# Moving a table's angles to integers on one engine and its sines ahead of the products, in an FFT filter followed by a feed-forward layer

## The chip, the cores and the metric

The kernel runs on one core of a Trainium2 chip. The metric is the device time of one execution in microseconds (us). "Span" is the time from the first to the last instruction in the profiler's records; the device time is longer than the span, most often by 2.0 or 2.1 us.

## The reference, cut to what matters

```python
def _attn_ref(x, filt_r, filt_i):              # x: 8 x 3008 x 256, filters 1505 x 256
    X = np.fft.rfft(x, axis=1)
    F = (filt_r + 1j * filt_i)[None, :, :]
    return np.fft.irfft(X * F, n=x.shape[1], axis=1).astype(np.float32)

def _moe_ref(x, w_in, w_out, beta):            # 24064 tokens, 256 -> 2048 -> 256
    h = x @ w_in
    g = h * (1.0 / (1.0 + np.exp(-beta * h)))
    return (g @ w_out).astype(np.float32)
```

The kernel does the transforms as matrix products with tables of sines and cosines, in two steps each way. It builds the tables on the chip at its start. `t2`, the second table, is the large one: 24 blocks of 64 columns in five copies (cosine, cosine, sine, sine, minus cosine). The first batch item goes through the whole transform (the "head", 36 us), and then the **main stage** begins: feed-forward matmuls on TensorE with a SiLU on ScalarE for each of 752 steps, into which the transforms of batch items 1 to 7 are woven.

## The kernel before

The angles of half 0 of `t2` are computed on VectorE and those of half 1 on GpSimd, in fp32 turns, and rounded with the usual add-and-subtract of a large constant:

```python
ROUND_C = 1.5 * (2**23)
def angles(h, eng):
    u = setup.tile([P, NH, M], F32, ...); r = setup.tile([P, NH, M], F32, ...)
    eng.tensor_tensor(u[:], ka[...half h, broadcast...], kb[...broadcast...], ALU.add)
    eng.tensor_scalar(r[:], u[:], ROUND_C, ROUND_C, ALU.add, ALU.subtract)
    eng.tensor_tensor(u[:], u[:], r[:], ALU.subtract)

def t2_part(h, part):                       # all on ScalarE, 128x768 or 2 x 128x384
    if part == 0:   nc.scalar.activation(t2[:, ks_, 2, :], u[:], ACT.Sin, scale=TWO_PI)
    elif part == 1: nc.scalar.activation(r[:], u[:], ACT.Abs)
    else:           # two cosines, as sines of r with a bias of half pi
        ...
angles(0, nc.vector)
angles(1, gp)
```

`first1(i, on_act)` multiplies four rows of `x` for one of eight blocks and evacuates two psum tiles into `a_t`, each by ScalarE or VectorE; `warm(n)` is n matmuls on zeros that keep TensorE busy. ScalarE does half 1 of the table only among the products:

```python
for i in range(2):
    first1(i, (True, True))
    warm(2 if i == 0 else 8)
t2_part(0, 0)
first1(2, (False, False)); warm(2)
for part in (1, 2): t2_part(0, part)
first1(3, (False, False)); warm(2)
t2_sin(0, nc.vector); t2_more(0)            # copies and negation on VectorE
first1(4, (False, False)); warm(2)
first1(5, (True, True)); warm(2)
first1(6, (True, True)); warm(1)
first1(7, (False, True))
...                                          # turn_a: transposes of a_t, evacuated
product(0)
TAB = (1, 2, 5, 6, 8, 9)
for i in range(NK // 2 + FLAG):              # NK // 2 = 12 products, 2 multiplies each
    if 0 < i < NK // 2: product(i)           # VectorE: nc.vector.tensor_tensor(..., ALU.mult)
    ...
    if i < 3:  t2_part(1, i)
    if i in TAB: table3(...)                 # a table's transposes, evacuated
    if i == 3:
        t2_more(1)
        for h in range(1, 4): load_wout(h)   # weights of the feed-forward layer
        load_x(1, X_HALVES[2:], xs[1])       # second halves of batch item 1
        ...
    if i >= FLAG: inverse3(i - FLAG)
```

Two places in the main stage turn out to matter. The work woven into it is placed by step number, and the filter loads `uf` are issued on the same queue (SyncE) as the stores of the results, which leave from a pool of three staging buffers:

```python
ostp = pool("ostp", 3)
...
at = place(9, 14, units[J // 4 :], per=9)
place(at + 1, at + 1, [lambda: a2_read(1)] + uf(JG, NK), per=9)   # steps 15 and 16: 8 filter loads
...
if fb == NFB - 1:                                   # a block of 512 rows is done
    for h, a in enumerate(acc):
        if h * per % 2 == 0:
            ost = ostp.tile([P, 2, D], F32, name="ost", tag="ost")
        on_act = h == 0 and i < 6 or last and h % 2 == 0
        evac(ost[...], a[:], on_act)                # ScalarE or VectorE
        eng = nc.scalar if last and h >= 2 else nc.sync
        store(..., ost[...], eng)
```

## Time and profile before

| | before |
|---|---|
| device time, median of 3 | 782.55 us (782.0 to 783.15) |
| span of the profiled execution | 780.9 us |
| busy share: TensorE, ScalarE, VectorE, GpSimd | 99%, 76%, 50%, 19% |
| first multiply of the products starts | 16.27 us |
| last (24th) multiply starts | 32.00 us |
| first SiLU (start of the main stage as ScalarE sees it) | 36.38 us |
| last SiLU starts | 775.68 us |

### The profile page before, as it was taken

The page shows a single profiled execution, that of the slowest core. Times are in us where ns is not written, and L with a number is a line of the kernel's source. Part 1 is how long each engine was busy: PE and PEld are TensorE (multiplying, and loading weights), DVE is VectorE, ACT ScalarE, POOL GpSimd, SP SyncE. Part 2 cuts the span into 40 slices and gives each one's busy share as a digit, 9 for nine tenths or more (in the row PEclk, how much of TensorE's full clock was granted, in tenths as well). Part 3 has the DMA queues.
Part 4 walks back from the last instruction along what each step waited for, and adds up shares of the span by engine and source line. Part 5 has one row for each costly group of instructions (what it writes and reads, how often), then busy time and mean ns, then how long its engine had stood idle before and what let it go on. Part 6 is the DMA issues. An engine that isn't in the chain of part 4 may idle for free.

```text
span 780.9 us, 15549 instructions
## 1 busy us (share of the span) xinstructions
PE 772.5 (99%) x6111; PEld 549.0 (70%) x6111; DVE 392.8 (50%) x644; ACT 594.3 (76%) x922; POOL 145.3 (19%) x144
## 2 busy tenths in 40 slices
PE   9999999999999999999999999999999999999998
PEld 5767667766777667876668766787677776776665
DVE  8847846746446563475635746277452761500101
ACT  6987886886678867787677876778767787677776
POOL 8522501420013100231002310024000330000000
PEclk9999999999999999999999999999999999999999
DMA  9978674517801186022850239412371114100101
GB/s 187 245 188 229 155 211 134 127 68 202 222 28 68 69 209 195 29 81 96 196 167 28 96 114 183 148 56 81 120 206 43 61 68 128 55 29 28 55 28 55
DMA packets 84185, 91.46 MB, mean 117 GB/s; under 512 B 4498, under 2 KB 74276, under 8 KB 83154
## 3 DMA queue, kind: packets, MB, share of 16 engines
q1 hardware_dynamic: 81008, 73.95, 30.9%
q0 software_dynamic: 2816, 16.26, 10.7%
q8 instruction: 48, 0.79, 0.4%
q10 hardware_dynamic: 288, 0.26, 0.1%
q14 instruction: 25, 0.20, 0.1%
HBM read 57.16 MB, written 46.66 MB: 133 GB/s over the span
## 4 chain that ended last, share of the span: by engine, by line
PE 95%; DVE 2%; ACT 1%; issue 1%; DVEq 0%
PE acc L877 42%; PE hps L835 41%; PE ps L626 3%; PE ps L551 3%; PE ps L674 2%; PE ps L648 2%; PE pw L187 1%; DVE qb_t L451 0%; DVE a_t L109 0%; ACT a L107 0%; DVE q_t L660 0%; PE pz L543 0%; DVE q_t L663 0%; DVE p_t L659 0%; ACT z_t L107 0%
## 5 line engine op out<-in xcount | busy, mean ns | idle before, releaser
L844 ACT ACTIVATE gT<-hps,beta_sb 128x512 bf16<-128x512 f32 x752 | 515.4, 687 | 174.0 <-PE hps L835 163.3
L877 PE MATMUL acc<-wout_sb,gT 128*128 128x256 bf16 x3008 | 451.4, 272 | 0.0
L835 PE MATMUL hps<-y,win_sb 128*128 128x512 bf16 (+8 forms) x1730 | 447.8, 351 | 0.3 <-ACT gT L844 0.3
L877 PEld LDWEIGHTS <-gT 128*128 128x128 bf16 x3008 | 285.7, 98 | 128.1 <-ACT gT L844 0.2
L835 PEld LDWEIGHTS <-win_sb 128*128 128x128 bf16 x1730 | 164.9, 98 | 24.7 <-issue 0.6
L664 POOL TENSOR_TENSOR v_t<-p_t,q_t 128x512 bf16<-128x512 f32 x84 | 106.7, 1270 | 387.7 <-DVE q_t L663 377.6
L109 DVE COPY ost<-acc 128x512 f32<-128x512 f32 (+1 forms) x88 | 56.2, 677 | 193.2 <-PE acc L877 188.8
L109 DVE CAST a<-ps 96x512 bf16<-96x512 f32 x96 | 65.9, 687 | 86.3 <-PE ps L626 84.8
L111 DVE TENSOR_SCALAR y<-ps 128x376 bf16<-128x376 f32 (+1 forms) x119 | 63.8, 544 | 61.2 <-PE ps L551 61.2
L659 DVE TENSOR_TENSOR p_t<-ps,frr 128x512 f32<-128x512 f32 x84 | 58.1, 691 | 29.9 <-PE ps L648 28.0
L663 DVE TENSOR_TENSOR q_t<-ps,fri 64x512 f32<-64x512 f32 x84 | 58.3, 694 | 1.2
L660 DVE SCALAR_TENSOR_TENSOR q_t<-ps,fri 64x512 f32<-64x512 f32 x84 | 57.5, 684 | 1.1
L551 PEld LDWEIGHTS <-zz 96*128 96x128 bf16 x512 | 35.3, 97 | 28.9
L107 ACT ACTIVATE z<-ps 128x512 bf16<-128x512 f32 x84 | 49.5, 589 | 0.6 <-PE ps L674 0.6
L626 PE MATMUL ps<-xg,t 94*96 94x512 bf16 x112 | 41.9, 381 | 0.1
L551 PE MATMUL ps<-t,zz 96*128 96x94 bf16 x448 | 36.7, 204 | 0.0
L674 PE MATMUL ps<-v_t,t 128*128 128x256 bf16 x168 | 32.1, 273 | 1.0 <-DVE q_t L663 1.0
L648 PE MATMUL ps<-a,t 128*128 128x256 bf16 x168 | 32.1, 273 | 0.0
L118 POOL DMA_DIRECT2D xg<-in_x_dram x22 | 12.0, 550 | 100.1 <-PE acc L877 96.8
L648 PEld LDWEIGHTS <-t 128*128 128x128 bf16 x168 | 15.8, 98 | 14.4
L626 PEld LDWEIGHTS <-t 94*96 94x96 bf16 x112 | 13.6, 123 | 11.9
L674 PEld LDWEIGHTS <-t 128*128 128x128 bf16 x168 | 16.1, 98 | 7.8 <-DVE q_t L663 1.8
(121 smaller groups left out, 196.8 us busy)
## 6 DMA issues: line engine op xcount, KB each, us to landing
out_dram<-ost SPq DMA_DIRECT2D x80, 256.0 KB
d<-a SPq DMA_DIRECT2D x28, 384.0 KB
a<-d SPq DMA_DIRECT2D x28, 384.0 KB
d<-z SPq DMA_DIRECT2D x28, 384.0 KB
zz<-d SPq DMA_DIRECT2D x28, 384.0 KB
xg<-in_x_dram POOLq DMA_DIRECT2D x6, 1280.0 KB, 10.1
frr<-in_filt_r_dram SPq DMA_DIRECT2D x12, 256.0 KB
out_dram<-ost SPq DMA_DIRECT2D x18, 128.0 KB
```

What stands on the lines that cost most here:

```text
L109: nc.vector.tensor_copy(dst, src)
L111: nc.vector.tensor_scalar_mul(dst, src, scale)
L551: nc.tensor.matmul(ps[:, e, :NP], lhsT=zz[:, jj + e, dc * P : (dc + 1) * P], rhs=tab[:], start=True, stop=True,)
L626: nc.tensor.matmul(ps[:KP], lhsT=t1[:], rhs=s["x"][:, 2 * i : 2 * i + 2, :], start=True, stop=True)
L648: nc.tensor.matmul(ps[:, e, :], lhsT=t2[:, k0 + e, 3:5, :].rearrange("p c k -> p (c k)"), rhs=s["a2"][g][:, kk + e, :], start=True, stop=True,
L659: nc.vector.tensor_tensor(p_t[:], ps[:], frr[:, ks_, :], ALU.mult)
L663: nc.vector.tensor_tensor(q_t[:M], ps[M:P], fri[M:P, ks_, :], ALU.mult)
L664: nc.gpsimd.tensor_tensor(v_t[:], p_t[:], q_t[:], ALU.add)
L674: nc.tensor.matmul(ps[:, e, :], lhsT=t3[:, k0 + e, :], rhs=v_t[:, e, :], start=True, stop=True)
L835: nc.tensor.matmul(hps[:, pos - t0 : pos - t0 + ln], lhsT=win_sb[:, dc, fb * P : (fb + 1) * P], rhs=ys[b][:, dc, n0 : n0 + ln], start=(dc ...
L844: nc.scalar.activation(gT[:, :tn], hps[:, :tn], ACT.Silu, scale=beta_sb[:, fb : fb + 1])
L877: nc.tensor.matmul(acc[tb // per][:, tb % per, :], lhsT=g_[:, tb * P : (tb + 1) * P], rhs=wout_sb[:, f_, :], start=(f_ == 0 and tb % per = ...
```

## The change

The intent: take the angle work off slow GpSimd, make it cheaper on VectorE (the remainder of a turn is one bit operation on integers), and have all sines of the table done before the products, so that ScalarE evacuates for the products undisturbed. GpSimd gets the copies. Cut to its core:

```diff
+TURN = 2**22
...
-    angles(0, nc.vector); angles(1, gp)          # add, round, subtract
+    for h in range(2):
+        u = setup.tile([P, NH, M], I32, name="u", tag=f"u{h}")
+        nc.vector.tensor_tensor(u[:], ka[...], kb[...], ALU.add)
+        nc.vector.tensor_scalar(u[:], u[:], TURN - 1, None, ALU.bitwise_and)
...
-            nc.scalar.activation(t2[:, ks_, 2, :], u[:], ACT.Sin, scale=TWO_PI)
+            nc.scalar.activation(t2[:, ks_, 2, :], u[:], ACT.Sin, scale=TWO_PI / TURN, bias=pi[:])
-            nc.scalar.activation(r[:], u[:], ACT.Abs)
+            nc.scalar.activation(r[:], u[:], ACT.Abs, scale=1.0 / TURN, bias=half[:])
...
+    first1(0, (True, True));   warm(2);  t2_part(0, 0)
+    first1(1, (False, False)); warm(8);  t2_part(0, 1); t2_part(0, 2); t2_copy(0, 3, 2)
+    ...                                            # keep, on GpSimd
+    t2_copy(0, 0, 1)
     first1(2, (False, False)); warm(2)
+    first1(3, (True, True));   warm(2)
+    nc.vector.tensor_scalar_mul(t2[:, :NH, 4, :], t2[:, :NH, 1, :], -1.0)
+    t2_part(1, 0)
+    first1(4, (False, False)); warm(1)
+    t2_part(1, 1)
+    first1(5, (False, True));  warm(1)
+    first1(6, (False, True));  first1(7, (False, True))
...
+    t2_part(1, 2)
+    t2_copy(1, 3, 2); t2_copy(1, 0, 1)             # GpSimd
+    gp.tensor_tensor(t2[:, NH:, 4, :], zeros, t2[:, NH:, 1, :], ALU.subtract)
...
-        if i < 3: t2_part(1, i)
-            table3(1 + n // 2, 2 - 2 * (n % 2), n % 2 == 0 or n == 5)()
+            table3(1 + n // 2, 2 - 2 * (n % 2), n % 2 == 0)()
```

More of the change, by code (lines that the diff above doesn't have):

```diff
@@ L242 @@
     hm = fixed("hm", -0.5 * math.pi)
+    pi = fixed("pi", -math.pi)
+    half = fixed("half", -0.5)
     ms = small("ms")
     nc.vector.tensor_scalar(ms[:], q_p[:], float(J), j_p[:], ALU.mult, ALU.add)
-    nc.vector.tensor_scalar_mul(ms[:], ms[:], 1.0 / S)
+    nc.vector.tensor_scalar_mul(ms[:], ms[:], float(TURN) / S)
     off2 = small("off2")
-    nc.vector.tensor_scalar(off2[:], c_p[:], -0.25, 0.25, ALU.mult, ALU.add)
+    nc.vector.tensor_scalar(off2[:], c_p[:], -0.25 * TURN, 0.75 * TURN, ALU.mult, ALU.add)
     ka = setup.tile([P, NK], F32, name="ka", tag="ka")
@@ L257 @@
     NH = NK // 2
-    us, rs = [], []
-    def angles(h, eng):
-        u = setup.tile([P, NH, M], F32, name="u", tag=f"u{h}")
-        r = setup.tile([P, NH, M], F32, name="r", tag=f"r{h}")
-        eng.tensor_tensor(
+    us = []
+    for h in range(2):
+        u = setup.tile([P, NH, M], I32, name="u", tag=f"u{h}")
+        nc.vector.tensor_tensor(
             u[:],
@@ L268, in angles @@
         )
-        eng.tensor_scalar(r[:], u[:], ROUND_C, ROUND_C, ALU.add, ALU.subtract)
-        eng.tensor_tensor(u[:], u[:], r[:], ALU.subtract)
+        nc.vector.tensor_scalar(u[:], u[:], TURN - 1, None, ALU.bitwise_and)
         us.append(u)
-        rs.append(r)
+    rs = [setup.tile([P, NH, M], F32, name="r", tag=f"r{h}") for h in range(2)]
     def t2_part(h, part):
@@ L277, in t2_part @@
         if part == 0:
-            nc.scalar.activation(t2[:, ks_, 2, :], u[:], ACT.Sin, scale=TWO_PI)
+            nc.scalar.activation(
+                t2[:, ks_, 2, :], u[:], ACT.Sin, scale=TWO_PI / TURN, bias=pi[:]
+            )
         elif part == 1:
-            nc.scalar.activation(r[:], u[:], ACT.Abs)
+            nc.scalar.activation(r[:], u[:], ACT.Abs, scale=1.0 / TURN, bias=half[:])
         else:
@@ L285, in t2_part, with t2_copy @@
                 )
-    def t2_sin(h, eng):
+    def t2_copy(h, dst, src):
         ks_ = slice(h * NH, (h + 1) * NH)
-        eng.tensor_copy(t2[:, ks_, 3, :], t2[:, ks_, 2, :])
-    def t2_more(h):
-        ks_ = slice(h * NH, (h + 1) * NH)
-        nc.vector.tensor_scalar_mul(t2[:, ks_, 4, :], t2[:, ks_, 1, :], -1.0)
-        nc.vector.tensor_copy(t2[:, ks_, 0, :], t2[:, ks_, 1, :])
-    m_p = small("m_p")
-    gp.tensor_scalar(m_p[:], ip_f[:], float(M), float(-M), ALU.is_ge, ALU.mult)
-    gp.tensor_tensor(m_p[:], m_p[:], ip_f[:], ALU.add)
-    keep = small("keep")
-    gp.tensor_scalar(keep[:], m_p[:], -1.0, float(M - 1), ALU.mult, ALU.add)
-    gp.tensor_tensor(keep[:], keep[:], m_p[:], ALU.mult)
-    gp.tensor_scalar(keep[:], keep[:], 0.5, 0.5, ALU.is_gt, ALU.mult)
-    angles(0, nc.vector)
-    angles(1, gp)
-    id_f = setup.tile([NFB, NFB], F32, name="id_f", tag="id_f")
-    gp.tensor_copy(id_f[:], ident[:NFB, :NFB])
-    tiny = setup.tile([NFB, P], F32, name="tiny", tag="tiny")
-    gp.tensor_tensor(tiny[:], bt[:], bt[:], ALU.mult)
-    gp.tensor_scalar(tiny[:], tiny[:], 1e-12, 2e-6, ALU.is_lt, ALU.mult)
-    gp.tensor_tensor(bt[:], bt[:], tiny[:], ALU.add)
-    gp.tensor_copy(
-        t1.rearrange("p (a k) -> p a k", a=4), t1b.rearrange("p (k a) -> p a k", a=4)
-    )
+        gp.tensor_copy(t2[:, ks_, dst, :], t2[:, ks_, src, :])
     a_t = ypool.tile([P, NDC, NK, J, 4], BF16, name="a_t", tag="y")
@@ L339, in first1 @@
             )
-    for i in range(2):
-        first1(i, (True, True))
-        warm(2 if i == 0 else 8)
+    first1(0, (True, True))
+    warm(2)
     t2_part(0, 0)
+    first1(1, (False, False))
+    warm(8)
+    t2_part(0, 1)
+    t2_part(0, 2)
+    t2_copy(0, 3, 2)
+    m_p = small("m_p")
+    gp.tensor_scalar(m_p[:], ip_f[:], float(M), float(-M), ALU.is_ge, ALU.mult)
+    gp.tensor_tensor(m_p[:], m_p[:], ip_f[:], ALU.add)
+    keep = small("keep")
+    gp.tensor_scalar(keep[:], m_p[:], -1.0, float(M - 1), ALU.mult, ALU.add)
+    gp.tensor_tensor(keep[:], keep[:], m_p[:], ALU.mult)
+    gp.tensor_scalar(keep[:], keep[:], 0.5, 0.5, ALU.is_gt, ALU.mult)
+    t2_copy(0, 0, 1)
     first1(2, (False, False))
     warm(2)
-    for part in (1, 2):
-        t2_part(0, part)
+    first1(3, (True, True))
+    warm(2)
+    nc.vector.tensor_scalar_mul(t2[:, :NH, 4, :], t2[:, :NH, 1, :], -1.0)
+    t2_part(1, 0)
+    first1(4, (False, False))
+    warm(1)
+    t2_part(1, 1)
+    first1(5, (False, True))
+    warm(1)
+    first1(6, (False, True))
+    first1(7, (False, True))
     def table3(i, part, on_act, own=None):
@@ L364, in go @@
                 return
-            if part:
-                evac(dst[:, 0, :], pt[:, 0, :], on_act, 0.5)
-            else:
-                nc.vector.tensor_scalar_mul(dst[:, 0, :], pt[:, 0, :], keep[:])
+            evac(dst[:, 0, :], pt[:, 0, :], on_act, 0.5 if part else keep[:])
             evac(dst[:, 1:KG, :], pt[:, 1:KG, :], on_act)
         return go
-    first1(3, (False, False))
-    warm(2)
-    t2_sin(0, nc.vector)
-    t2_more(0)
-    first1(4, (False, False))
-    warm(2)
-    first1(5, (True, True))
-    warm(2)
-    first1(6, (True, True))
-    warm(1)
-    first1(7, (False, True))
     tabs = [
-        table3(0, 0, False, fpsum.tile([P, KG, P], BF16, name="pt", tag="f")),
+        table3(0, 0, True, fpsum.tile([P, KG, P], BF16, name="pt", tag="f")),
         table3(0, 2, True, hpsum.tile([P, KG, P], BF16, name="pt", tag="hps")),
     ]
-    for go in tabs:
-        go()
+    t2_part(1, 2)
+    t2_copy(1, 3, 2)
+    t2_copy(1, 0, 1)
+    gp.tensor_tensor(
+        t2[:, NH:, 4, :],
+        wz[:, :M].unsqueeze(1).broadcast_to([P, NH, M]),
+        t2[:, NH:, 1, :],
+        ALU.subtract,
+    )
+    id_f = setup.tile([NFB, NFB], F32, name="id_f", tag="id_f")
+    gp.tensor_copy(id_f[:], ident[:NFB, :NFB])
+    tiny = setup.tile([NFB, P], F32, name="tiny", tag="tiny")
+    gp.tensor_tensor(tiny[:], bt[:], bt[:], ALU.mult)
+    gp.tensor_scalar(tiny[:], tiny[:], 1e-12, 2e-6, ALU.is_lt, ALU.mult)
+    gp.tensor_tensor(bt[:], bt[:], tiny[:], ALU.add)
+    gp.tensor_copy(
+        t1.rearrange("p (a k) -> p a k", a=4), t1b.rearrange("p (k a) -> p a k", a=4)
+    )
     a2s = []
@@ L426 @@
     turn_a(1, True)
+    for go in tabs[::-1]:
+        go()
     z_t = ypool.tile([P, NDC, J, KP], BF16, name="z_t", tag="y")
@@ L500 @@
             turn_a(2 + 2 * (i // 3) + i % 3, True)
-        if i < 3:
-            t2_part(1, i)
         if i == 0:
-            t2_sin(1, gp)
             late_loads()
@@ L507 @@
             n = TAB.index(i)
-            table3(1 + n // 2, 2 - 2 * (n % 2), n % 2 == 0 or n == 5)()
+            table3(1 + n // 2, 2 - 2 * (n % 2), n % 2 == 0)()
         if i == 3:
-            t2_more(1)
             for h in range(1, 4):
```

## The prediction

> **What bounds the kernel now.** I read the page first (busy shares and the clock row), then the chain of waits in order of time for the first 38 us, then busy time by stage, then each engine's timeline there, then the waits of TensorE after it. From the page:
>
> ```profile
> PE 772.5 (99%) x6111; PEld 549.0 (70%) x6111; DVE 392.8 (50%) x644; ACT 594.3 (76%) x922; POOL 145.3 (19%) x144
> PEclk9999999999999999999999999999999999999999
> ```
>
> TensorE is busy 99% of the span at full clock. The tables that this change touches are built only before the first feed-forward matmul of the main stage (L835 at 35.74 us). So the change can only move the moment at which that stage begins: at most a few of 36 us, against 15.65 us that 2% would need. The chain of waits there (start, us, what):
>
> ```profile
> 10.31 1.95 DVE a_t L109 x4
> ...
> 13.17 1.33 DVE a_t L109 x3
> ...
> 14.84 0.40 DVE t3b L109
> ...
> 15.25 0.57 DVE a L109
> ...
> 17.64 0.73 ACT t L278
> 18.37 0.70 ACT a L107
> 19.07 0.73 ACT r L280
> 19.80 0.70 ACT t L107
> 20.50 1.00 ACT t L283 x2
> ```
>
> Up to 15.8 us the end hangs on VectorE's evacuations, then until 22.7 us on ScalarE. There the second half's sine (L278), absolute value (L280) and two cosines (L283) take 0.73 + 0.73 + 1.00 = 2.46 us between evacuations that the products wait for. That is what the change takes out. Busy time by stage (PE, PEld, DVE, ACT, POOL):
>
> ```profile
> 14.50:16.80 2.30, 1.99 (x29) 1.72 (x27) 1.82 (x5) 1.74 (x4) 2.30 (x3) 1.00 1.18 259
> 16.80:22.70 5.90, 4.79 (x62) 4.05 (x61) 5.90 (x13) 5.87 (x10) 3.38 (x9) 1.00 1.08 235
> 22.70:31.50 8.80, 8.60 (x122) 8.08 (x121) 8.56 (x16) 8.60 (x16) 5.72 (x9) 1.00 1.08 228
> ```
>
> The reader is to see that ScalarE is not alone: VectorE is busy 5.90 of 5.90 us in the middle row. The chain names one engine where two are full. GpSimd's timeline:
>
> ```profile
> 7.99 0.94 POOL L298 TENSOR_SCALAR m_p<-ip_f 128x1 f32<-128x1 f32 x1
> 10.05 1.46 POOL L263 TENSOR_TENSOR u<-ka,kb 128x768 f32<-128x768 f32 x1
> 11.60 2.81 POOL L269 TENSOR_SCALAR r<-u 128x768 f32<-128x768 f32 x1
> 14.49 1.81 POOL L270 TENSOR_TENSOR u<-u,r 128x768 f32<-128x768 f32 x1
> 18.43 0.82 POOL L289 COPY t<-t 128x768 bf16<-128x768 bf16 x1
> 20.88 0.18 POOL L418 COPY held<-fri 32x1 f32<-32x1 f32 x1 [1.63 <-DMA fri<-in_filt_r_dram]
> ```
>
> GpSimd is the reason that the second half is late (its angles end at 16.3 us). It then waits for a filter load at 20.88 us before it may issue the weight loads.
>
> **What the Trainium skill says.** "VectorE: DVE Perf Modes", § The perf-mode tier table: fp32 tensor_tensor runs at 1x, tensor_scalar in SBUF at 2x. The trace agrees: 0.96 us for the 128x768 add, 0.56 for the 128x768 tensor_scalar. The integer bit operations on 128x96 take 0.20 us, as do the fp32 ones, so I give the new 128x768 mask 0.56 us. "ScalarE: Activation LUTs", § What ACT_TABLE_LOAD costs: a per-partition pointer operand adds about 93 ns. The trace agrees: the 128x768 sine without one takes 0.85 us, 0.64 of it elements by the page's 0.833 ns, so 0.21 fixed; the 128x384 cosine with a bias pointer takes 0.62, so 0.30 fixed. "SBUF — State Buffer", § Who interferes with whom: a VectorE instruction with two SBUF inputs or in a two-port mode shuts GpSimd out for its length. The trace fits: m_p takes 0.94 us against 0.19 for the next ones, and ends just after VectorE's subtraction (7.87 to 8.83).
>
> **The change, part by part.**
>
> *Angles.* VectorE did add, round, subtract for half 0 (0.96, 0.56, 0.96). Now it does add and mask for both halves: by the start-to-start steps of the trace 0.99 + 0.60, twice. It starts at 6.34 (two more 0.03 us memsets), so half 0 is ready at 7.9 instead of 8.8, and VectorE is free at 9.5 instead of 8.8. GpSimd loses 6.1 us of angle work.
>
> *ScalarE before the products.* It evacuates the first block at 7.46 and 7.85, then the half-0 sine at 8.24 (was 9.00), absolute value at 9.07, cosines at 10.04 and 10.56, done at 11.16 (was 11.73). Sine and absolute value now carry a bias pointer, 0.09 us more each. Then block 3 at 11.10 (TensorE's order up to here is as before, its psum is ready at 11.08) and 11.49, half-1 sine 11.88, absolute value 12.71, one evacuation each of blocks 5, 6, 7 at 13.55, 13.94, 14.33. The last ends at 14.82. Before, the last a_t evacuation ended at 14.67.
>
> *VectorE before the products.* Block 1 at 9.51 and 9.98 (0.47 a step), block 2 at 10.45, the negation 0.27 at 11.39, block 4 at 11.86 and 12.33, one each of blocks 5 to 7, ended by 14.3. The two 128x768 copies (0.38 + 0.27) and the table evacuation (0.68, 14.56 to 15.24) leave VectorE. So it idles when the transposes of a_t come. They start at 14.9 (was 14.71, for ScalarE's 14.82), and VectorE's evacuation of the first starts at 15.4 (was 15.25). The first product is multiplied at 16.4 (was 16.27). The three warm-up matmuls that go (0.22 us each) buy nothing here: TensorE waits for the evacuations. So far the change is 0.13 us behind.
>
> *ScalarE in the products.* It has from 14.72: cosines of half 1 (1.02), transpose evacuation (0.70) to 16.44, table part 2 (0.77) to 17.21, table part 0 (0.86, it came from VectorE) to 18.07, three evacuations of 0.70 to 20.17, and is at the first inverse result by 20.3 (was 21.39). It is ahead by 1.1 us.
>
> *VectorE in the products.* Here the sum is: 24 multiplies of 0.603 = 14.47 us; table evacuations before 2 x 0.47, now 3 (the one of the last group comes over from ScalarE); negation and copy of half 1 before 0.54, now none; idle before 0.41. Before: 14.47 + 0.94 + 0.54 + 0.41 = 16.36, and 16.27 + 16.36 = 32.63, as the trace has it (32.68). Now: 14.47 + 1.41 = 15.88 if it never waits, and 16.40 + 15.88 = 32.28. Following the psum buffers, I get multiplies ready just before VectorE wants them: product 2 by 0.2 us, 3 by 0.07, 4 by 0.12, 5 by 0.12. So no stall, but no margin. Gain 0.35 us.
>
> *After it.* The rest of the chain to 35.74 follows the last multiply and shifts whole. TensorE's waits after 36 us:
>
> ```profile
> PE ps L674 <- DVE q_t L663: 1.0, 2, 0.7
> PE hps L835 <- ACT gT L844: 0.3, 1, 0.3
> ```
>
> 1.3 us in 744, none for a load: the first weights are scaled at 35.99 and used at 37.99, so a start up to 2 us earlier costs no new wait. The shift carries to the end. 782.55 - 0.35 = 782.2.
>
> **The rivals.**
> - *ScalarE was the bound.* The chain for 16.8 to 22.7 us says so, and 2.46 us leave that stretch while 0.86 come in: a gain of up to 1.6 us, 781.0. Against it stands VectorE's full row: whatever ScalarE gives back before 22.7 us, VectorE must still do 24 multiplies back to back.
> - *ScalarE becomes the bound earlier.* It runs from 11.1 to 20.2 us without a pause, with the products' first psum buffers held by the table transposes, which it evacuates only at 17.2 and 18.1 (was 14.8 to 15.7 by two engines). If an int32 input, which no row of this trace shows on ScalarE, or the pointers cost 0.1 us more per instruction, the products start 0.3 to 0.5 us later: 782.6 to 783.0.
> - *GpSimd becomes the gate.* Its copies of half 1 wait for the cosines at 15.8: 0.8, then the two-input subtraction at 1.5 to 1.8 (from L263 and L270), then 2.0 us of small ones, at the filter wait by 20.4. That load comes at 20.88, so nothing moves; 1 us of blocking would delay the weights by 0.5 us, still inside the 2 us of slack. Time 782.2 all the same.
> - *The shift is lost later.* VectorE sets the end from 67 to 75 us; if its work there hangs on loads whose time is fixed by the queue, TensorE waits 0.35 us longer: 782.55.
>
> **Range and chances.** First and second rival pull about equally, each perhaps one in four. With runs of one kernel spread over 1.15 us, I take 781.4 to 783.0. Faster by 2% would need 15.65 us from a phase of 36 us whose loads do not move: 0.005. Slower by 2%: only through a large fault such as the clock dropping: 0.01.
>
> **What would show each step.** Right: half-0 sine at about 8.2 us, last a_t evacuation at about 14.8, first multiply at about 16.4, no sine or absolute value after 16.5, ScalarE's first z_t at about 20.3, VectorE with under 0.2 us idle from 16.4 to 32.3, L835 at about 35.4, weight loads issued at 21.9 as before. Wrong: the first multiply before 16.0 or after 16.9; VectorE idle by more than 0.4 us among the products (then ScalarE or psum buffers were the bound); sines of int32 input much over 0.94 us; a wait of TensorE for wout_sb; TensorE's waits after 36 us grown by the gain.

## The result, and the profile after

| | before | after |
|---|---|---|
| device time, median of 6 | 782.72 us (782.0 to 783.15) | 783.44 us (782.25 to 784.43) |
| span of the profiled execution | 780.9 | 782.2 |

The ratio is 1.001, with a 95% interval of 0.9997 to 1.0023: the same, at 2%. Here and below a ratio is the mean time of one kernel's runs over that of the other's of the same rounds, so not quite the ratio of the medians quoted. Executions over 1.5% slower than the fastest of the same kernel are left out of the means. The class was as predicted, but 783.44 is above the range of 781.4 to 783.0. The question is why a head start of 0.35 us became a loss of 0.7.

The page of the changed kernel (busy us, share and instructions of each engine; granted clock in 40 slices):

```profile
PE 766.8 (98%) x6012; PEld 548.4 (70%) x6108; DVE 393.0 (50%) x644; ACT 594.5 (76%) x921; POOL 142.5 (18%) x145
PEclk9999999999999999999999999999999999999999
```

Nothing shows there. (Of the 99 fewer TensorE instructions three are the warm-up matmuls; the rest are records that the trace has lost, as the weight loads, 6108 against 6111, show.) First the chain of waits in the head of this first trace after (start, us, what):

```profile
3.19 7.17 DMA xg<-in_x_dram
...
11.65 0.87 ACT a_t L109 x2
12.52 0.82 ACT t L280
13.34 0.82 ACT r L284
14.16 1.14 ACT a_t L109 x3
```

The head hangs on a load of `x` that was issued at 3.19 us and landed at 10.37, where the trace of before had it at 9.29. Behind it stand, in ScalarE's program order, block 3's two evacuations (until 12.52), then half 1's sine, then its absolute value, then the last evacuations. A second execution of the changed kernel (after_again, below) had the load at 9.22, and its stages look as the prediction had drawn them (PE, PEld, VectorE, ScalarE, GpSimd busy us, in the same windows as the prediction's table of before):

```profile
14.50:16.80 2.30, 1.82 (x23) 1.59 (x24) 1.18 (x3) 2.30 (x6) 1.13 (x2) 1.00 1.18 260
16.80:22.70 5.90, 5.42 (x75) 4.81 (x73) 5.90 (x12) 5.72 (x10) 4.47 (x10) 1.00 1.07 238
22.70:31.50 8.80, 8.27 (x120) 7.70 (x118) 8.80 (x17) 7.40 (x15) 5.80 (x9) 1.00 1.07 228
```

VectorE is now busy for the whole of both product rows (before 5.90 and 8.56), and ScalarE has 1.2 us less to do in the last. GpSimd's own timeline in that execution (its new subtraction, and the copy that waits for the filter load):

```profile
16.46 1.64 POOL L377 TENSOR_TENSOR t<-wz,t 128x768 bf16<-128x768 bf16 x1
20.59 0.18 POOL L420 COPY held<-fri 32x1 f32<-32x1 f32 x1 [0.51 <-DMA fri<-in_filt_r_dram]
```

So GpSimd is no gate: it still waits for the load. The waits of TensorE after 36 us, in the first trace after:

```profile
PE ps L674 <- DVE q_t L663: 0.6, 2, 0.3
PE hps L835 <- ACT gT L844: 0.3, 1, 0.3
```

The first line was 1.0 us before: TensorE's waits of the main stage are not fixed. (They are not set by its start alone either: before_again below starts it at the same moment as before and has 0.3.) VectorE at 76 us explains it. In the brackets is the idle time just before and what ended it; first before, then after:

```profile
76.31 0.69 DVE L109 COPY ost<-acc 128x512 f32<-128x512 f32 x1 [1.44 <-DMA out_dram<-ost]
```

```profile
75.96 0.69 DVE L111 COPY ost<-acc 128x512 f32<-128x512 f32 x1 [0.98 <-DMA out_dram<-ost]
```

VectorE wants to evacuate the second half of the second block's result, but all three staging buffers still wait for their stores. The multiplies behind it in VectorE's program order start only after it (the first at 77.03 us before), and TensorE waits for them. The store queue (SyncE) in the trace of before tells why:

```profile
65.44 0.31 SPq L134 DMA_DIRECT2D frr<-in_filt_r_dram  x1
66.75 11.50 SPq L810 DMA_DIRECT2D out_dram<-ost  x10
```

The first block's results were in their buffers at 58.64 us (VectorE's copy of 57.95 plus 0.69). Their five stores are issued only from 66.75 on, after eight filter loads that stand ahead of them, the last at 65.44. Whatever the head gains, these stores do not move with it: in the seven traces with this order of the queue they start at 65.65 to 68.13, and at 65.65 in both before_again and after_pad3, whose main stages start 0.75 us apart.

Last, the end of the program: ScalarE's issue of the last two stores, before and after, and the DMA queues between 776 and 783 us after.

```profile
777.43 0.89 ACTq L796 DMA_DIRECT2D out_dram<-ost  x2
```

```profile
777.09 2.40 ACTq L796 DMA_DIRECT2D out_dram<-ost  x2
...
q8 instruction: 1, 0.02, 1.2%
```

The same two issues took 2.40 us instead of 0.89, with one fetch of instructions beside them (queue q8). From the last SiLU to the end of the span it is 6.85 us in this trace and 5.17 to 5.19 in the sixteen others of the table below.

This gives the sum for the two first traces, from 780.86 to 782.19, a difference of +1.33: first multiply later by 0.76 (17.03 against 16.27), products shorter by 0.57 (15.16 against 15.73), so first SiLU later by 0.19; main stage shorter by 0.53 (738.77 against 739.30), end longer by 1.67. Two of the four are no work of the change on the face of it. That is what the experiments had to sort out.

### The profile page after: what moved, and what is told of

Same layout as the page of the kernel before. It is cut to its first block, busy times and chain, and to the rows that moved or that the text cites. A ratio compares the mean times of both kernels' runs of the same rounds, so it can differ in the third digit from the quotient of the medians.

```text
span 782.2 us, 15445 instructions
## 1 busy us (share of the span) xinstructions
PE 766.8 (98%) x6012; PEld 548.4 (70%) x6108; DVE 393.0 (50%) x644; ACT 594.5 (76%) x921; POOL 142.5 (18%) x145
## 4 chain that ended last, share of the span: by engine, by line
PE 94%; DVE 1%; ACT 1%; issue 1%; DMA 1%; POOL 0%; DVEq 0%; POOLq 0%
PE acc L877 43%; PE hps L835 38%; PE ps L626 3%; PE ps L551 3%; PE ps L674 2%; PE ps L648 2%; DMA xg<-in_x_dram 1%; PE psz L472 0%; DVE q_t L660 0%; ACT a L109 0%; PE pz L543 0%; DVE q_t L663 0%; DVE qb_t L455 0%; DVE p_t L659 0%; ACT a_t L109 0%
## 5 line engine op out<-in xcount | busy, mean ns | idle before, releaser
L835 PE MATMUL hps<-y,win_sb 128*128 128x512 bf16 (+8 forms) x1636 | 427.4, 350 | 0.5 <-ACT gT L844 0.3
```

Of the source, the lines that this page charges most:

```text
L835: nc.tensor.matmul(hps[:, pos - t0 : pos - t0 + ln], lhsT=win_sb[:, dc, fb * P : (fb + 1) * P], rhs=ys[b][:, dc, n0 : n0 + ln], start=(dc ...
```

## The experiments

Sixteen kernels ran, in five rounds each. The theories:

- **Pin.** The change does start the main stage earlier, but the stores behind the filter loads fix a moment at about 75 us, so the lead is lost there. Rival: the change gains nothing in the head.
- **Late x.** In some executions the first loads of `x` land late and delay the changed kernel's head. Rivals: both kernels would suffer alike; or the late landing is only a symptom.
- **VectorE bounds the products**, as predicted. Rival: ScalarE does.
- **Place of the instructions.** The slow last store comes from where a fetch of instructions falls, which three fewer matmuls moved. (The texts of the first four runs call this theory C.) Rival: one execution's accident.

The table has the moments of each trace, in us. "x" is the landing of the fourth load of x. "Main stage" is from the first SiLU to the last. The rows are grouped by what stands in the queues.

| trace | x | first multiply | last multiply | first SiLU | VectorE's evacuation near 75 us | main stage | last SiLU |
|---|---|---|---|---|---|---|---|
| before | 9.29 | 16.27 | 32.00 | 36.38 | 76.31 | 739.30 | 775.68 |
| before_again | 9.64 | 16.28 | 32.00 | 36.39 | 74.95 | 738.39 | 774.78 |
| before_less3 | 9.38 | 16.29 | 32.02 | 36.40 | 76.03 | 739.00 | 775.40 |
| after | 10.37 | 17.03 | 32.19 | 36.57 | 75.96 | 738.77 | 775.34 |
| after_again | 9.22 | 16.18 | 31.41 | 35.79 | 76.92 | 740.51 | 776.30 |
| after_pad3 | 9.28 | 16.03 | 31.26 | 35.64 | 74.95 | 738.69 | 774.33 |
| after_third | 10.23 | 16.74 | 32.08 | 36.47 | 76.55 | 739.46 | 775.93 |
| before_sf | 9.26 | 16.27 | 32.00 | 36.38 | 74.82 | 738.40 | 774.78 |
| after_sf | 9.33 | 16.08 | 31.30 | 35.69 | 74.50 | 738.78 | 774.47 |
| after_sf_t1 | 9.22 | 16.07 | 30.83 | 35.22 | 73.65 | 738.40 | 773.62 |
| after_sf_t3 | 9.13 | 15.91 | 31.09 | 35.47 | 74.44 | 738.94 | 774.41 |
| before_np_again | 9.31 | 16.39 | 32.12 | 36.50 | 74.92 | 738.39 | 774.89 |
| after_np | 10.05 | 16.56 | 31.79 | 36.17 | 74.60 | 738.40 | 774.57 |
| after_np_again | 9.26 | 16.07 | 31.30 | 35.68 | 74.10 | 738.38 | 774.06 |
| after_np_t1 | 10.33 | 16.84 | 31.61 | 35.99 | 74.42 | 738.40 | 774.39 |
| before_np_xlate | 9.91 | 16.71 | 32.44 | 36.82 | 75.25 | 738.40 | 775.22 |
| after_np_xlate | 10.49 | 17.01 | 32.23 | 36.61 | 75.03 | 738.39 | 775.00 |

Three readings carry the rest. Last multiply to first SiLU is 4.38 or 4.39 in every row. First to last multiply is 15.72 to 15.73 in every row of the kernel before and 15.16 to 15.34 with the change (mostly 15.22 or 15.23; the t1 and t3 rows, which split the work otherwise, apart). And the main stage is 738.38 to 738.40 wherever nothing is waited for, and longer, by up to 2.12, where something is.

### Both kernels again

No edit: more executions and one more trace of each.

> The kernel before, unchanged, for a second trace. Theory A (the difference of the two first traces lies in two things that vary from execution to execution, the landing of the first x loads and the issue of the last output store): this trace differs from the first one of the same kernel by as much as 1 us in the landing of the x chunk issued at 3.19 us (9.29 in the first trace, 10.37 in the changed kernel's) or in the last store's issue (0.47 against 1.96 us), and the five times spread over about 1 us. Theory B (both come from the change): x lands at 9.3 +- 0.2, the last store's issue takes 0.5 us, and the last SiLU comes at 775.7 +- 0.2 as in the first trace.

> The changed kernel, unchanged, for a second trace. Theory A (chance): x chunk at about 9.3 or 10.4 as it falls; when the first multiply is not held by x it comes at 16.4 +- 0.2 instead of 17.03 and the last SiLU at 775.0 instead of 775.34; the last store's issue 0.5 or 2 us. Theory B (the change does it): x at 10.4 +- 0.2, first multiply at 17.0, last store's issue 2 us and an instruction fetch beside it, median 0.7 us over the kernel before.

**Measured:** before_again 782.53 us (ratio to before 0.9998, 0.9986 to 1.0011), after_again 782.81 (1.0005, 0.9992 to 1.0017), so the same. In the traces the changed kernel starts its main stage 0.60 us earlier than before_again (35.79 against 36.39) and still ends it 1.52 us later (776.30 against 774.78): VectorE's evacuation of the second block starts at 76.92 in the one and at 74.95 in the other, where it had waited for a store for only 0.2 us. The last store took its normal time in both.

**What follows:** the lead in the head is real, and it is lost between 36 and 77 us. The evacuation and the last SiLU move together: measured from the trace of before, the last SiLU is 0.62 later for an evacuation 0.61 later (after_again) and 0.34 earlier for one 0.35 earlier (after), and the main stage's start counts for nothing in either. One reservation: in after_again the record puts the wait down to a TensorE result (2.7 us) and not to a store, and in before_less3 below to a ScalarE one (1.2 us). A wait for several is put down to the one that the record has last, so these two do not show the store by themselves; the moved queue further down does, for the wait as a whole.

### The place of the instructions

after_pad3 puts three small matmuls back into the changed kernel, and before_less3 takes three out of the kernel before:

```diff
 # after_pad3
     warm(8)
+    warm(3, 16)
 # before_less3
     first1(4, (False, False))
-    warm(2)
+    warm(1)
     first1(5, (True, True))
-    warm(2)
+    warm(1)
     first1(6, (True, True))
-    warm(1)
```

> The changed kernel with three tiny extra warm-up matmuls (16 columns) after the block of eight, where TensorE waits for x anyway, so that TensorE has as many instructions as in the kernel before and its last instruction fetch falls at the same place of the program. If the slow last store comes from where the program's end lies against the fetches (theory C): last store's issue 0.5 us, last fetch at 775 rather than 777.7, time about 1 us less than the changed kernel. If by chance: same as the changed kernel within 0.3 us in the mean.

> The kernel before with only the three warm-up matmuls taken out that the change takes out. Theory C (place of the fetch): last fetch at about 777.7, last store's issue about 2 us, time about 1 us over the kernel before. Otherwise within 0.3 us of the kernel before; main stage not earlier by more than 0.1 us, since the products wait for VectorE and not for TensorE.

**Measured:** after_pad3 783.16 us median (781.53 to 783.59; ratio 1.0008, 0.9994 to 1.0022), before_less3 783.12 (782.46 to 783.77; 1.0005, 0.9993 to 1.0018). The last store was normal in both traces, and it was normal in after_again too, which had nothing put back.

**What follows:** the theory is neither shown nor out. The packets in the traces bear out its first half. In the five traces of the kernel before with all its warm-up matmuls the 48th fetch on queue q8 starts at 773.9 to 775.0 us, ahead of the last stores. In before_less3 it starts at 781.1, after the end of the span. With the change it comes at 777.7 or later, or not at all, in ten of eleven traces (after_pad3, none, is one of the ten; after_sf_t1 has 773.5). Only in the first trace after, at 777.73, does it fall into the issue of the last stores, and only there are they slow: one trace of the seventeen in the table. What makes them slow stays open.

The record shows one more cost at the end that the spans do not hold. In 6 of the 56 executions with the change the device time is 2.7 to 3.5 us longer than the span; in the other 50, and in 66 executions without it, it is at most 2.3. Chance alone would put all six on one side about once in a hundred times. One of the six is of after_pad3, so putting three matmuls back does not mend it; its cause is open as well.

after_pad3 and before_less3 are of more use as two further draws of the pin: evacuation at 74.95 and 76.03, last SiLU 1.35 earlier and 0.28 earlier than in the trace of before, where the evacuation was 1.36 and 0.28 earlier.

### The changed kernel a third time

> The changed kernel unchanged, a third trace. Theory P: last SiLU pinned to the moment at which VectorE's second output evacuation (76 us) gets its buffer, with the same offset as in the five traces before (699.36 us later, +- 0.05), whatever the first SiLU's time; mean time within 0.5 us of the kernel before. Rival: last SiLU follows the first SiLU's time.

**Measured:** 781.98 us (ratio 0.9997, 0.9985 to 1.001). x landed at 10.23, the first multiply came at 16.74, the evacuation at 76.55 after waiting 1.7 us for a store, and the last SiLU 0.25 us after that of before, for an evacuation 0.24 later. Last store normal.

**What follows:** measured from the first trace of before, the last SiLU follows the evacuation one for one, within 0.02 us, in five of the six other traces with the old queue order, whatever the first SiLU does. The sixth, before_again, hardly waited there (0.2 us) and has the bare 738.39.

### The filter loads behind the stores

In both kernels the eight filter loads go to step 18, after the first block's stores. No other line is touched, but the placing by step then also moves two of four small negations on VectorE by one step (its copy of the first block's result comes at 57.35 us instead of 57.95, long before the stores leave):

```diff
-        place(at + 1, at + 1, [lambda: a2_read(1)] + uf(JG, NK), per=9)
+        place(at + 1, at + 1, [lambda: a2_read(1)], per=9)
+        place(18, 18, uf(JG, NK), per=12)
```

> The kernel before with one thing moved in the main stage: the first block's output stores go to the queue ahead of the eight later filter loads, so that the output buffer that VectorE wants at 76 us is free in time. Theory P (the pin: in the first 76 us the main stage is held by a buffer whose release is timed by the queue, so whatever the first stage gains is swallowed there): VectorE waits under 0.3 us for the buffer, the last SiLU comes at 774.8 +- 0.2 instead of 775.68 in the first trace, the time is 0.3 to 0.8 us lower than the kernel before. Rival Q (no pin; the gain was never there): no change beyond 0.2 us.

> The changed kernel with the same move of the first stores. Theory P: with the pin gone the 0.6 to 0.75 us that the change gains before the first SiLU reach the end: last SiLU 774.1 +- 0.2, 0.7 earlier than in the kernel before with the same move, time lower than that one by 0.4 to 0.8 us. Rival Q: same as the kernel before with the same move within 0.2 us.

**Measured:** before_sf 781.97 us (781.75 to 782.32; ratio 0.9997, 0.9984 to 1.001), its spans 780.0 to 780.1. after_sf 781.9 us (781.19 to 783.87; 0.9999, 0.9987 to 1.0012), its spans 779.1 to 781.7. SyncE's queue in before_sf:

```profile
59.54 3.72 SPq L811 DMA_DIRECT2D out_dram<-ost  x5
63.43 0.46 SPq L131 DMA_DIRECT2D frr<-in_filt_r_dram  x1
```

The stores leave 7.2 us earlier (59.54 against 66.75), VectorE's evacuation waits for none, and the kernel before gets its main stage down to 738.40 from 739.30:

```profile
74.82 0.69 DVE L109 COPY ost<-acc 128x512 f32<-128x512 f32 x1
```

The changed kernel starts 0.69 us ahead of before_sf but ends its main stage only 0.31 ahead, and by device time the two cannot be told apart (0.4 to 0.8 us had been expected). What took the rest is in its TensorE waits (the list of waits, then the timeline):

```profile
PE ps L626 <- DMA xg<-in_x_dram: 0.2, 1, 0.2
...
46.29 0.60 PE L626 MATMUL ps<-xg,t 94*96 94x512 bf16 x2 [0.22 <-DMA xg<-in_x_dram]
```

This pair of matmuls starts 1.63 us after the matmul of the same line before it, against 1.26 in before_sf: 0.37 of the 0.38 us that are lost.

**What follows:** the pin is shown: with the queue's order changed and no other line, the wait goes in both kernels and a lead of 0.31 us survives. But there is a second pin. Until 46.29 us TensorE waits for the second half of batch item 1's x, which landed at 46.16. That load is issued behind three loads of weights, and in the eleven traces with this order it lands anywhere from 44.6 to 46.6 us. The earlier the main stage starts, the sooner it gets there; but chance has a part too (after_sf_t1 below starts earliest of all, has the load at 44.61 and does not wait).

### That load ahead of the last weights, too

```diff
         if i == 3:
-            for h in range(1, 4):
-                load_wout(h)
+            load_wout(1)
             if B > 1:
                 load_x(1, X_HALVES[2:], xs[1])
                 ...
+            for h in range(2, 4):
+                load_wout(h)
```

> The kernel before with two moves in the load and store queues: the first stores ahead of the filter loads (as in the earlier run) and the second half of batch 1's x ahead of two weight loads, so that it lands before 43 us instead of at 45 to 46.5. Theory P: no second wait was on its path, so it is like the run with the first move alone: last SiLU 774.8 +- 0.15, spans 780.0, times spread under 0.6 us. If the later weights become a wait: slower by that wait.

> The changed kernel with both moves. Theory P with its second pin (x of batch 1, which the earlier start reaches before it has landed: TensorE waited 0.2 us for it, and the lead shrank from 0.69 to 0.40): no wait of TensorE for x at 46 us, the lead of 0.65 to 0.75 us at the first SiLU is there at the last: 774.1 +- 0.15; mean time 0.6 to 0.8 us under the kernel before with both moves, unless first-x landings delay single executions. Rival: the lead is lost all the same, at most 0.3 us left.

> The kernel before with the later queue places once more, because the execution profiled last time was a freak at 2100 us. Last SiLU at 774.8 within 0.2, span 780.0 within 0.3, no wait of VectorE for an output store at 75 us. If the second halves of batch 1 had pinned this kernel too, the last SiLU would come earlier than the 774.78 of the version with the filter blocks moved alone.

> The changed kernel with the later queue places once more. Theory: the lead at the first SiLU over the kernel before with the same places, 0.65 to 0.75 us if the first chunks of x land by 9.7 us and 0.2 to 0.4 if they land after 10, is kept within 0.1 us to the last SiLU. Rival (a further pin in the main stage): a lead of 0.6 or more at the first SiLU shrinks to 0.4 or less at the last.

**Measured:** the execution of before_np that was profiled took 2100.5 us; its other four took 781.8 to 782.66 (ratio 0.9999, 0.9985 to 1.0012). The comparison needed a second pair. after_np 781.86 us (ratio 0.9993, 0.9979 to 1.0006). before_np_again 782.06 (0.9997, 0.9983 to 1.001), after_np_again 781.49 (0.9989, 0.9976 to 1.0001). The second halves now land between 40.7 and 42.3 us. TensorE's waits after 36 us in after_np_again, the whole list:

```profile
PE hps L837 <- ACT gT L846: 0.3, 1, 0.3
PE ps L675 <- DVE q_t L664: 0.3, 1, 0.3
```

before_np_again has the same two lines. Against it, after_np_again starts the main stage 0.82 us earlier (35.68 against 36.50) and ends it 0.83 earlier (774.06 against 774.89). after_np, with x late, starts 0.33 earlier and ends 0.32 earlier. The spans of five executions are 779.2 to 779.3 for after_np_again and 779.9 to 780.5 for before_np_again.

**What follows:** with both pins out, the whole lead is kept to 0.01 us, and the spans of these two runs do not overlap (their device times, 781.12 to 782.2 and 781.67 to 782.64, still do). Rival "the change gains nothing in the head" is out, and these traces show no third pin. The kernel before gained nothing from the second move (738.39 against 738.40), since its load had landed at 45.59 us in before_sf. It is not safe from the second pin: in the first trace of before the load landed at 46.56, and the matmuls that read it started 1.35 us after the one before them, 0.09 more than in before_sf.

### VectorE or ScalarE in the products

On top of the moved filter loads, one or all three of VectorE's table evacuations among the products (128x768) go to ScalarE:

```diff
-            table3(1 + n // 2, 2 - 2 * (n % 2), n % 2 == 0)()
+            table3(1 + n // 2, 2 - 2 * (n % 2), n % 2 == 0 or n == 5)()    # t1
+            table3(1 + n // 2, 2 - 2 * (n % 2), True)()                     # t3
```

> The same, and the last table evacuation (128x768, 0.47 us on VectorE, 0.70 on ScalarE) goes back to ScalarE, as it was before the change. If VectorE's back-to-back multiplies set the end of the product stage (the prediction's reading): first SiLU 0.45 us earlier than in the run above, 35.2, and time 0.4 lower. If ScalarE sets it (rival): no gain, or 0.2 us later.

> The same, with all three such evacuations on ScalarE (1.41 us off VectorE, 2.1 us more on ScalarE, which was 7.82 of 8.80 us busy in the second half of the products). VectorE alone the bound: first SiLU 1.4 us earlier than with none moved. Both engines near full: only 0.3 to 0.9 us earlier, about like the run above, since ScalarE becomes the bound.

> Both moves, and the last table evacuation on ScalarE. Theory P and VectorE as the bound of the products: lead at the first SiLU 1.1 to 1.2 us and kept: last SiLU 773.6 +- 0.15, mean time 1.0 to 1.3 us under the kernel before with both moves and 1.5 under the kernel before.

**Measured:** after_sf_t1 781.76 us (ratio 0.9996, 0.9983 to 1.001), after_sf_t3 781.58 (0.9991, 0.9978 to 1.0003), after_np_t1 781.66 (0.9992, 0.9979 to 1.0004). In the traces, first to last multiply goes from 15.22 (after_sf) to 14.76 in after_sf_t1 and 14.77 in after_np_t1, but is 15.18 in after_sf_t3.

**What follows:** one evacuation less on VectorE shortens the products by 0.46 us, which is its start-to-start step of 0.46 us. VectorE was the bound, without a margin on the other side: with all three on ScalarE, VectorE waits 0.58 and 0.34 us among the products for matmuls of TensorE, which has itself just waited 0.21 us for an evacuation by ScalarE. ScalarE is busy 5.90 of 5.90 us in the middle stage, and nearly all of the gain is gone. The first of VectorE's two waits in after_sf_t3:

```profile
20.17 0.69 DVE L455 TENSOR_TENSOR pb_t<-ps,fri 128x512 bf16<-128x512 f32 x1 [0.58 <-PE ps2q L446]
```

after_sf_t1 has the shortest span, 778.8 us, 2.1 below the first trace of before, but its five executions lie at 778.8 to 780.5. after_np_t1 fell short of what was expected: with x at 10.33 its lead over before_np_again is 0.51 us at the first SiLU instead of 1.1 to 1.2, and 0.50 at the last.

### Late x on purpose

One more memset on GpSimd, ahead of its issue of the first loads, in both kernels with both pins out:

```diff
+    late = setup.tile([P, 1024], F32, name="late", tag="late")
+    nc.gpsimd.memset(late[:], 0.0)
     x_cur = load_x(0, X_FIRST)
```

> The kernel before with the later queue places (filter blocks at 18, second halves of batch 1 ahead of the last weights), plus one GpSimd memset ahead of the issue of the first loads of x, which should make the first x chunks and the first filter group land about 0.9 us later. Theory (the change used up the slack that hid late first loads): here the first multiply moves by at most 0.2 us from its 16.27, because three more warm-up matmuls stand ahead of the x matmuls, and the span stays at 780.0 to 780.5. Rival (first loads set the first multiply in both kernels alike): the first multiply moves by about as much as in the changed kernel.

> The changed kernel with the later queue places and the same memset. Theory: the first multiply goes from the 16.03 to 16.18 of its early traces to 16.6 to 17.0, as in its four late traces, and the first SiLU and the last one come later by 0.4 to 0.8 us, so span about 780.2 and no lead left over the kernel before. Rival one (both alike): the same shift in both kernels. Rival two (the late loads were a symptom, not the cause): the first multiply stays within 0.2 us of 16.1.

**Measured:** before_np_xlate 782.55 us (ratio 1.0002, 0.999 to 1.0015), after_np_xlate 782.38 (0.9999, 0.9986 to 1.0011). The loads were issued 0.61 and 0.59 us later, less than the 0.9 estimated. The fourth load of x landed at 9.91 in the one (0.60 later than in before_np_again) and at 10.49 in the other (1.23 later than in after_np_again), so the doses were not the same. The first multiply came 0.32 us later (16.71 against 16.39) and 0.94 later (17.01 against 16.07). The chains, first of before_np_xlate, then of after_np_xlate:

```profile
10.05 0.34 PE psa L330 x4
...
10.41 1.95 DVE a_t L109 x4
```

```profile
10.63 0.50 PE psa L307 x8
...
11.77 0.87 ACT a_t L109 x2
12.64 0.82 ACT t L282
```

**What follows:** "only a symptom" is out: load x late and the changed kernel's first multiply is late, as in its naturally late traces (16.56 to 17.03 for landings of 10.05 to 10.37). The size that I expected for the kernel before (at most 0.2 us) is wrong too, at 0.32. Part of both is the memset itself: half 0's sine starts 0.30 us later in before_np_xlate (9.29 against 8.99) and 0.25 later in after_np_xlate (8.30 against 8.05), before x comes into it. If that passes through whole, which was not tested, what is left is 0.02 us in the kernel before, for x 0.60 late, and 0.69 in the changed one, for x 1.23 late. The doses differ, so the runs don't show how much of that second number the kernel before would have suffered. They do show the path in the changed one: ScalarE waited 0.55 us for block 3's psum, and half 1's sine and absolute value stood behind that wait in its program order. In the kernel before, that sine comes at 17.5 us or later, in the products, and ScalarE has nothing of half 1 waiting behind the blocks.

## Why the prediction was wrong, point by point

**Right: what bounds.** VectorE's single angle instructions took what was estimated: the integer mask on 128x768 0.56 us and the add 0.96. (The four together took 2.93 us in after_again, not 3.18, so VectorE was free at 9.22 us and not at 9.5.) The sines of integer input took 0.94 us and the absolute values 0.92 to 0.93, as the estimate with a bias pointer had it. The products took 15.23 us from first to last multiply plus the last one's 0.68, so 15.91 against the predicted 15.88, with VectorE busy throughout. First to last multiply against before, that is 0.50 us gained. The rival "ScalarE was the bound" fell with after_sf_t1. GpSimd was no gate, and the weight loads were issued at 21.69 us in after_again, predicted 21.9. ScalarE's first z_t came at 20.02, predicted 20.3. The rest of the head shifted whole, at 4.38 us. (One gap in the argument did no harm: the page that the prediction cites for VectorE shutting GpSimd out limits the case of two SBUF inputs to GpSimd instructions that read SBUF. The instruction that it was read from, m_p, does.)

**Wrong in size: the first multiply.** The step was "Then block 3 at 11.10 (TensorE's order up to here is as before, its psum is ready at 11.08)", which led to a last a_t evacuation at 14.82 and a first multiply at 16.4. In after_again block 3's evacuation started at 10.95, half 1's sine at 11.71 rather than 11.88, the last evacuation ended at 14.61, and the first multiply came at 16.18. In the other traces with early x it came at 15.91 to 16.08, earlier than in any trace of the kernel before (16.27 at the least). So the head gained 0.6 to 0.8 us where 0.35 was predicted, when x is early. Where x landed after 10 us, block 3's evacuation came at 11.33 to 11.77, and the first multiply at 16.56 to 17.03. The prediction gave ScalarE's new order a risk only from slow integer input or bias pointers; that the new order put the table behind a load was not in it.

**The step that failed: "so a start up to 2 us earlier costs no new wait. The shift carries to the end."** It was argued from two readings of the kernel before: TensorE's waits after 36 us are small, and the first weights are ready 2 us before use. Both are true and neither is enough. A wait of 1.0 us for VectorE's multiplies was on that list, and VectorE's wait had a store as its cause. That store's time is set by a queue and not by the head. In the unmoved kernels the last SiLU follows that moment one for one, and the moment itself scatters from 74.95 to 76.92 us. The last rival, "The shift is lost later", named the place (VectorE from 67 to 75 us) and the kind (work timed by the queue) and got 782.55. It was the right one, with two corrections: what VectorE waits for is a store behind loads, and not a load; and the moment varies by more than the gain. Behind it stood a second wait of the same kind, a half of x that lands at 46 us.

**The range.** It came from three runs of the kernel before, spread over 1.15 us. The changed kernel's first six spread over 2.2 us. The sum for its first trace has a late x, a lead lost to the pin, and one slow last store of 1.67 us. In two later calls the same kernel had medians of 782.81 and 781.98, both inside the range, so the 783.44 is in part an unlucky draw. It also holds two executions with 2.74 and 2.88 us between span and device time, a cost that only the change shows; with the usual 2.05 for these two, the median would be about 783.0 (an estimate from the six spans). All this comes on top of a prediction whose center was off for another reason: unmoved, the change is worth nothing that its own scatter does not cover.

**What stays open.** Why x lands late: counted from its issue, the fourth load took 6.07 to 6.45 us in all six usable traces of kernels without the change and 5.94 to 6.15 in six of eleven with it, but 6.72 to 7.18 in the other five. It is issued at the same moment (3.17 to 3.20 us, without the memset), and the memset pair had the late landing on the changed side only. That may be chance or the change; no run here tells which. Why the last store was slow in one trace, why about 1 us more is lost after the span in about one of nine executions with the change, and why one execution took 2100 us, is open as well.

**A version below both.** The changed kernel with both moves (after_np_again: 781.49 us, spans 779.2 to 779.3) is 0.9 us below the kernel before of its call by the medians (782.38, spans 780.0 to 781.1), and 0.6 below the kernel before with both moves (782.06). Its spans lie apart from those of both, its device times (781.12 to 782.2) overlap with theirs. The gain is 0.1%, and the interval of its ratio (0.9976 to 1.0001) just reaches no difference.

## What to carry to other kernels

Before you count a gain in an opening phase as a gain of the whole, list what in the next phase is timed by a queue and not by the phase before, and look at the stores as well as the loads: here a store issued behind a batch of loads held its buffer, the buffer held VectorE, which had multiplies behind that copy in its program order, and VectorE held TensorE. A list of small waits at the present start time does not say how long the waits are at an earlier one. A good test is the length of the next phase from its first to its last instruction: if it grows as its start moves earlier, something is pinned.

## What the Trainium skill lacked or had wrong

- "ScalarE: Activation LUTs", § What ACT_TABLE_LOAD costs, gives the cost of an instruction for fp32 and bf16 alike and says nothing of integer input. Here a 128x768 sine of int32 with a bias pointer took 0.94 us and one of fp32 without it 0.85: int32 costs nothing beyond the pointer's 93 ns, which that section has right.
- "VectorE: DVE Perf Modes", § The perf-mode tier table, has columns for bf16 and fp32 only (rates of 32-bit integer streams stand on another page, but none for an operation of this kind). A bit operation with a constant on 128x768 int32 took 0.56 us, as the fp32 tensor_scalar of the same size did in the kernel before, and an add of fp32 inputs written as int32 took 0.96, as the fp32 add.
- "TensorE: Matmul & The Clock Gate", § Part 1, tells of a half-rate clock, and that its end varies from execution to execution. Both agree: the 14 opening 128x512 matmuls first follow one another at 427 ns and then, in most traces, at 216, and the last of them started anywhere from 5.41 to 6.70 us. The half rate does not explain the 2100 us execution of before_np: there the 128x512 matmuls of the main stage follow one another at 621 ns (median). The trace of that execution holds no record of the clock, so the 1.000 that the profile prints for it is no measurement, and what slowed it stays open.
- I found no page that tells of the cost of an issue on ScalarE's store queue beside an instruction fetch: two issues took 2.40 us in one trace against 0.89, with one instruction packet beside them. One trace is all there is.
- I found no page that warns of what cost most here, the order of issue on SyncE: five stores whose data were ready at 58.64 us were issued from 66.75 on, after eight loads.
